# Reusing the maximum's turned score products as the first key tile, with one power of two per unit on GpSimd, in an attention and MLP block

## The chip, the cores and the metric

The kernel runs on one core of a Trainium2 chip. The metric is the device time of one execution in microseconds; the time of a kernel is the median of its runs.

## What is computed

The input `x` has 2048 tokens of width 448. The block adds three things: the input, an attention with 16 query heads of width 28 that share one key head and one value head, and an MLP of hidden width 1792. Both branches read the layer norm of `x`; the MLP normalizes once more.

```python
xn = _layernorm(x)
# attention: H = 16, Dh = 28, one k and one v for all heads
q = (xn @ wq).reshape(B, S, H, Dh).transpose(0, 2, 1, 3); k = xn @ wk; v = xn @ wv
scores = einsum("bhqd,bkd->bhqk", q, k) * Dh ** -0.5
o = einsum("bhqk,bkd->bhqd", softmax(scores), v)      # then heads side by side, @ wo
# MLP
y = _layernorm(xn); h = gelu(y @ w1 + b1); m = h @ w2 + b2
out = x + o @ wo + m
```

## The kernel before

The core has five engines with a queue each: PE multiplies matrices, ACT (ScalarE) evaluates functions, DVE (VectorE) and POOL (GpSimd) do elementwise work, SP (SyncE) issues most transfers. Each engine takes its own instructions strictly in the order in which the Python code issues them; semaphores make one engine wait for another. The schedule is written by hand: the loops call small jobs in turn.

There are three stages. First the norms and the projections to queries, keys and values; the queries go to DRAM (`qd`) as a high and a low part. Then the MLP, in slots of one 128-wide block of the hidden layer (`ft`) for 512 tokens (`c`), with the second product three slots behind the first. Last the attention, which begins some 354 us into the execution.

Attention is cut into 16 units. A unit is 512 queries of four heads (`j` = 0 to 3). The keys are cut into 16 tiles of 128 (`kt`). `score(u, kt, j)` makes one product of 128 keys by 512 queries on PE, into one of seven PSUM banks (`m`), and ACT takes the exponential of it into SBUF (`p`), so that keys lie on partitions. `pv(u, kt)` multiplies the four exponentials of a key tile by the values, into the one bank `po`, which also holds the sums of the exponentials (the values have a column of ones).

A unit takes eight steps, 0 to 7, of two key tiles. In a step the letters of a string say what is issued in turn: `s` a score, `m` a piece of work on maxima, `e` the end of that work, `n` a piece of the closing work of the unit before, `o` a piece of the output projection, `P` the value products of two key tiles (one step behind the scores).

The exponent needs a shift for each query, so that it doesn't overflow. The kernel uses the largest score over the first 128 keys. `max_jobs(u)` multiplies the queries of the unit by these keys (`km`) once more, as a product of its own: a score product of key tile 0, without the shift, since the rows that carry the shift are still empty. DVE turns each product in blocks of 32 by 32 (`tt`), and takes the largest of each block's rows (`mr`). `load_max(u)` joins the blocks, and SP sends the negative maxima, as a high and a low part, into two spare rows of the query tile `xh`. The score products then come out shifted. At the end `judge` looks whether all sums stayed in range; if not, a slow general path repeats the work (it is not taken with these inputs).

The closing work, `norm_jobs`, copies `po` to `oc`, squares it into a check sum, turns it, divides, and splits it into a high part `oth` (DVE) and a low part `otl` (POOL). The output projection of four units (`o_part`) reads these. Per unit there are 64 score products, 4 maximum products and the value products of 16 key tiles.

Of the kernel before, what the change touches and what calls it, by code (L numbers as in the profile page):

```python
# [15 lines left out]
P = 128  # L16
S, D, H, DH, F = 2048, 448, 16, 28, 1792
NT = S // P
CT = 4
# [4 lines left out]
EPS = 1e-5  # L24
SCALE = DH ** -0.5
BURST = 2
PAIRS = 12
# [11 lines left out]
def block_kernel(ctx, tc, x, wq, wk, wv, wo, w1, b1, w2, b2, out):  # L39
# [4 lines left out]
    def f(t):  # L44
        return t.bitcast(F32)
# [61 lines left out]
    def mtile(shape):  # L107
        return mp.tile(shape, F32, name="m")
# [344 lines left out]
    def load_q(u, blocks=range(4)):  # L453
        c, g = units[u]
        cols = slice(c * CW, (c + 1) * CW)
        if u < 2 and 0 in blocks:
            qst.append(xt_p.tile([P, 4, CW], F32R, name="xh"))
            pool.memset(f(qst[u]), 0.0)
# [9 lines left out]
    mrs = {}  # L468

# [9 lines left out]
    def load_max(u):  # L479
        while mxs.step():  # L480
            pass
        mb = mrs.pop(u)
# [10 lines left out]
        for h, r in ((0, 60), (1, 124)):  # L493
            for k in range(2):
                nc.sync.dma_start(f(qss[u][r:r + 1, 2 * k:2 * k + 2, :]), f(mn[:, h, k]))

    def max_jobs(u):
        mrs[u] = keep.tile([P, 4 * NT], F32, name="mr2", bufs=2)
        for j in range(4):
            pm = mtile([P, CW])  # L500
            pe.matmul(pm, km, qss[u][:, j, :], start=True, stop=True)  # L501
# [3 lines left out]
            dve.tensor_reduce(mrs[u][:, NT * j:NT * j + NT], tt.rearrange("p (b i) -> p b i", i=32), axis=AX.X, op=ALU.max)  # L505

# [15 lines left out]

    mxs, side, oside = Stream(), Stream(), Stream()

# [84 lines left out]
    ps = {}  # L609
    early = [(kt, j) for kt in range(2) for j in range(4)]  # L610

# [24 lines left out]
    for c in range(1, NCH):  # L636
        g = norm_gen(c, mtile)
        for i in range(CT + 1):
            norms[NF * (c - 1) + 5 + 2 * i] = lambda g=g: next(g, None)
    for n in range(len(mslots) + LAG):  # L640
        c, ft = mslots[n] if n < len(mslots) else (NCH, n - len(mslots))
# [10 lines left out]
        if (c, ft) == (NCH - 1, 7):  # L652
            load_q(0)
        if (c, ft) == (NCH - 1, 9):
            mxs.add(max_jobs(0))
        if (c, ft) == (NCH - 1, 12):
# [3 lines left out]
        for done, _ in enumerate(slot(n)):  # L660
            if done % 8 == 4 and (c, ft) in ((NCH - 1, 9), (NCH - 1, 10)):
                mxs.step()
            if c == NCH and done % 4 == 3 and early:
                score(0, *early.pop(0))
    assert not early
    ph1b.close()
# [15 lines left out]
    def prep_wo(g):  # L682
        pool.tensor_scalar(woh[:, g, :], wor[:, g, :], 1.0, 0.0, op0=ALU.mult, op1=ALU.add)
        pool.tensor_sub(wol[:, g, :], wor[:, g, :], f(woh[:, g, :]))

    rows = {}
# [140 lines left out]

    steps = [(u, kt) for u in range(NU) for kt in range(0, NT, 2)]
    pvq = [(u, kt) for u in range(NU) for kt in range(NT)]
    for n, (u, kt) in enumerate(steps):  # L830
        if n == len(steps) - 14:
            load_rows_of(NCH - 1, range(CT))
        if 4 <= n < 4 + NG:
            prep_wo(n - 4)
        if u and u + 1 < NU and kt == 0:
            load_q(u + 1)
        if u + 1 < NU and kt == 6:
            mxs.add(max_jobs(u + 1))
        jobs = [(u, kt + k, j) for k in range(2) for j in range(4)] if n else []
        for what in ORDERS[n % 2]:  # L840
            if what == "s" and jobs:
                score(*jobs.pop(0))
            elif what == "m":
                mxs.step()
            elif what == "e":
                if kt == 12 and u + 1 < NU:
                    load_max(u + 1)
            elif what == "n":
                side.step()
            elif what == "o":  # L850
                if n == len(steps) - 1:
                    o_part(NCH - 1, 0, range(NG - 1))
                oside.step()
            elif what == "P":
                assert not jobs
                for _ in range(BURST if n else 0):
                    pv(*pvq.pop(0))
    assert pvq and all(u == NU - 1 for u, kt in pvq)
# [6 lines left out]
    def full_max(u):  # L865
        qs = qst[u % 2]
        c, g = units[u]
# [19 lines left out]
    def general():  # L887
        for u in range(NU):
            c, g = units[u]
            full_max(u)  # L890
            qs = qst[u % 2]
            po = op.tile([P, CW], F32, name="po")
# [52 lines left out]
```

## Time and profile before

| | us |
|---|---|
| median of 3 runs | 913.89 (913.73 to 914.26) |
| the profiled execution | 913.37 |
| its span, first to last instruction | 911.4 |

| engine | busy us | share of the span |
|---|---|---|
| PE, matmuls | 900.5 | 99% |
| PE, weight loads | 583.5 | 64% |
| DVE | 428.6 | 47% |
| ACT | 712.7 | 78% |
| POOL | 61.2 | 7% |

A line of a group reads: source line, engine, operation, output <- inputs, shapes, count, then busy time and the mean duration of one in ns, then the engine's idle time just before them and what ended it. A line of the timeline reads: start in us, length in us, engine, line, operation, tiles, count; in brackets how long the engine had been idle and what released it. A line of the chain of waits has a start, a length and an engine with its line. PE's matmuls overlap one another, so a duration is more than the distance from one to the next; the same holds for ACT.

### The profile page before, as it was taken

Reading aid. Unit: us, or ns where it says so; the run is one execution under the profiler, and the core shown is the slowest. Engines: PE = TensorE matmul, PEld = TensorE weight load, DVE = VectorE, ACT = ScalarE, POOL = GpSimd, SP = SyncE. Lnnn points to the kernel's source line nnn. Section 1 sums busy time; section 2 is a strip of 40 time slices with the busy share of each in tenths; the row PEclk is TensorE's granted clock in tenths of the full one; section 3 lists DMA queues with packets and bytes.
Section 4 is the critical chain, followed back from the end, with each engine's and each line's share of the span. In section 5 each row is a group of like instructions: output and inputs, shape, how many; then the busy total and the mean of one; then the engine's idle time right before and its main releaser. Section 6 shows DMA issues by size and latency. Waiting matters only on the chain.

```text
span 911.4 us, 13365 instructions
## 1 busy us (share of the span) xinstructions
PE 900.5 (99%) x5041; PEld 583.5 (64%) x5041; DVE 428.6 (47%) x872; ACT 712.7 (78%) x1366; POOL 61.2 (7%) x69
## 2 busy tenths in 40 slices
PE   9999999999999999999999999999999999999997
PEld 8778888888888886444444564444564444564445
DVE  6777786676576584244234233234232244231212
ACT  5787664655554547999999969999969999969993
POOL 5340000000000002100000000000000000000000
PEclk9999999999999999999999999999999999999999
DMA  9773112002002204101102201102201102212001
GB/s 299 214 215 110 61 61 81 21 21 81 21 21 54 58 2 127 42 1 41 42 2 71 61 32 42 42 2 70 64 32 41 42 2 62 62 41 82 3 1 44
DMA packets 36265, 54.00 MB, mean 59 GB/s; under 512 B 7766, under 2 KB 24852, under 8 KB 36196
## 3 DMA queue, kind: packets, MB, share of 16 engines
q1 hardware_dynamic: 34788, 52.53, 19.9%
q8 instruction: 41, 0.67, 0.3%
q10 hardware_dynamic: 1408, 0.57, 0.2%
q14 instruction: 28, 0.23, 0.1%
HBM read 37.40 MB, written 14.68 MB: 57 GB/s over the span
## 4 chain that ended last, share of the span: by engine, by line
PE 95%; DVE 2%; DMA 1%; ACT 1%; issue 0%; SPq 0%; POOL 0%; DVEq 0%; POOLq 0%; ACTq 0%
PE m L630 28%; PE po L812 26%; PE ph L171 12%; PE m L573 5%; PE m L570 5%; PE m L576 5%; PE m L501 2%; PE qp L171 2%; PE m L703 1%; PE m L704 1%; PE m L705 1%; PE ph L174 1%; PE ph L176 1%; PE m L389 1%; PE m L263 1%; DMA qd<-qe 1%
## 5 line engine op out<-in xcount | busy, mean ns | idle before, releaser
L631 ACT ACTIVATE p<-m 128x512 f32<-128x512 f32 x1016 | 503.1, 666 | 39.2 <-PE m L630 38.8
L630 PE MATMUL m<-xh,ks 128*128 128x512 f32 x1024 | 276.7, 405 | 0.8 <-DVE a L580 0.8
L630 PEld LDWEIGHTS m<-xh,ks 128*128 128x128 f32 x1024 | 184.6, 188 | 118.7 <-ACT p L631 83.4
L812 PE MATMUL po<-p,vs 128*32 128x512 f32 x2016 | 242.4, 598 | 0.0
L812 PEld LDWEIGHTS po<-p,vs 128*32 128x32 f32 x2016 | 52.6, 109 | 119.0 <-issue 117.6
L740 DVE COPY oc<-po 128x512 f32<-128x512 f32 x15 | 10.4, 693 | 246.9 <-PE po L812 246.9
L544 ACT ACTIVATE hz<-ph,b1s 128x512 f32<-128x512 f32 x54 | 37.2, 689 | 103.4 <-PE ph L176 103.4
L576 PE MATMUL m<-w2h,hl 128*128 128x448 f32 x224 | 82.9, 370 | 0.0
L573 PE MATMUL m<-w2l,hh 128*128 128x448 f32 x224 | 82.0, 366 | 0.0
L570 PE MATMUL m<-w2h,hh 128*128 128x448 f32 x224 | 81.8, 365 | 0.0
L504 DVE STREAM_TRANSPOSE tt<-m 128x512 f32<-128x512 f32 x64 | 45.8, 716 | 67.5 <-PE m L501 64.5
L171 PE MATMUL ph<-xh,w1h 128*128 128x512 f32 x162 | 63.4, 391 | 0.8 <-ACT hx L545 0.8
L171 PE MATMUL ph<-xl,w1h 128*128 128x512 f32 x162 | 63.5, 392 | 0.3 <-DVE xl L265 0.3
L171 PE MATMUL ph<-xh,w1l 128*128 128x512 f32 x162 | 63.4, 391 | 0.0
L546 DVE TENSOR_SCALAR hz<-hz 128x512 f32<-128x512 f32 x56 | 25.3, 452 | 59.8 <-ACT hz L544 59.5
L755 POOL TENSOR_TENSOR otl<-oc,oth 128x512 fp32r<-128x512 f32 x15 | 19.4, 1292 | 484.8 <-PE m L630 274.0
L550 ACT ACTIVATE hz<-hz 128x512 f32<-128x512 f32 x56 | 35.3, 630 | 17.2 <-DVE hz L547 17.2
L570 PEld LDWEIGHTS m<-w2h,hh 128*128 128x128 f32 x224 | 42.1, 188 | 4.8
L573 PEld LDWEIGHTS m<-w2l,hh 128*128 128x128 f32 x224 | 42.1, 188 | 4.6
L505 DVE TENSOR_REDUCE mr<-tt 128x16 f32<-128x512 f32 x64 | 43.9, 686 | 2.2
L576 PEld LDWEIGHTS m<-w2h,hl 128*128 128x128 f32 x224 | 42.1, 188 | 3.3
L547 DVE TENSOR_TENSOR hz<-hz,hx 128x512 f32<-128x512 f32 x56 | 38.8, 693 | 7.7 <-ACT hx L545 4.9
(170 smaller groups left out, 968.2 us busy)
## 6 DMA issues: line engine op xcount, KB each, us to landing
xh<-qd SPq DMA_DIRECT2D x64, 224.0 KB
a<-in_A_x_dram SPq DMA_DIRECT2D x32, 224.0 KB
qd<-qe SPq DMA_DIRECT2D x24, 256.0 KB
ad<-a SPq DMA_DIRECT2D x16, 224.0 KB
a<-ad SPq DMA_DIRECT2D x16, 224.0 KB
raw<-in_B_w_dram SPq DMA_DIRECT2D x7, 448.0 KB
out_dram<-a SPq DMA_DIRECT2D x14, 224.0 KB
raw<-in_B_w_dram SPq DMA_DIRECT2D x4, 336.0 KB
```

The lines of the kernel that those rows point to most:

```text
L171: pe.matmul(ps, w, v, start=(n == 0), stop=False)
L504: dve.transpose(tt, pm)
L505: dve.tensor_reduce(mrs[u][:, NT * j:NT * j + NT], tt.rearrange("p (b i) -> p b i", i=32), axis=AX.X, op=ALU.max)
L544: act.activation(hz, ph, AF.Square, bias=b1s[:, ft:ft + 1], scale=GELU[0] ** 0.5)
L547: dve.tensor_mul(hz, hz, hx)
L550: act.activation(hz, hz, AF.Tanh, scale=GELU[1])
L570: pe.matmul(m2[k], hh[:, ts], w2h[:, ft, :], start=(ft == 0), stop=False)
L573: pe.matmul(m2[k], hh[:, ts], w2l[:, ft, :], start=False, stop=False)
L576: pe.matmul(m2[k], hl[:, ts], w2h[:, ft, :], start=False, stop=(ft == NF - 1))
L630: pe.matmul(s, ks[:, kt * P:(kt + 1) * P], qss[u][:, j, :], start=True, stop=True)
L631: act.activation(p, s, AF.Exp, scale=SCALE)
L812: pe.matmul(po[32 * j:32 * j + 32, :], vs[:, kt, :], ps.pop((u, kt, j)), start=(kt == 0), stop=(kt == NT - 1))
```

## The change

The maximum products of a unit are the scores of key tile 0, only without the shift and turned. The change keeps them in `tt` and makes the exponentials of key tile 0 from them, so that tile 0 is no longer scored a second time:

- `first_shift(u, j)`: DVE subtracts the maximum from the turned product, by a broadcast of `mq`, a copy of the maxima on all partitions that `load_max` now makes.
- `first_exp(u, j)`: ACT takes the exponential in place. For j = 0 of units 1 to 15 the shift is in powers of two (scaled by `BITS`, written to `bits`) and POOL raises a tile of twos to it.
- `first_back(u, j)`: DVE turns the result back into `p0`, which the value products of key tile 0 read.

Since maxima must be complete before the shift, they are now taken two units ahead (a third query tile is added), one maximum product in each of steps 3 to 6. These four steps have seven scores and the others eight (`SHARES`; a unit has 60). `shift_jobs(u + 1)` runs in steps 2 to 7 of unit u and in step 0 of the next, in the places `X` and `Y`. For unit 1 it starts a step later and ends in step 1 of unit 1, behind the first turn of unit 0's `norm_jobs`. Unit 0's exponentials of tile 0 are made in the MLP's last slots, all four on ACT.

On PE, over steps 2 to 4 of a unit before (L630 scores, L812 value products, L501 maximum products):

```order
L630 MATMUL m<-xh,ks 128x512 x8
L812 MATMUL po<-p,vs 32x512 x8
L501 MATMUL m<-xh,km 128x512
L630 MATMUL m<-xh,ks 128x512 x2
L501 MATMUL m<-xh,km 128x512
L630 MATMUL m<-xh,ks 128x512 x2
L501 MATMUL m<-xh,km 128x512
L630 MATMUL m<-xh,ks 128x512 x4
L812 MATMUL po<-p,vs 32x512 x8
L501 MATMUL m<-xh,km 128x512
L630 MATMUL m<-xh,ks 128x512 x8
L812 MATMUL po<-p,vs 32x512 x8
```

And on PE over steps 1 to 3 of a unit after (L683 scores, L875 value products, L510 maximum products; `p_4257` is the unit's tile p0):

```order
L683 MATMUL m<-xh,ks 128x512 x8
L875 MATMUL po<-p_4257,vs 32x512 x4
L875 MATMUL po<-p,vs 32x512 x4
L683 MATMUL m<-xh,ks 128x512 x8
L875 MATMUL po<-p,vs 32x512 x8
L683 MATMUL m<-xh,ks 128x512 x3
L510 MATMUL m<-xh,km 128x512
L683 MATMUL m<-xh,ks 128x512 x4
```

A maximum product now takes the place of a score, and the first four value products of a unit read tile 0 from p0. (One row of value products counts the eight instructions of the program; the trace shows each as two.)

On DVE, from the end of the closing work of a unit into its step 4, before:

```order
L751 TENSOR_TENSOR oc<-oc,tr 128x512 [waits DVE_49]
L753 CAST oth<-oc 128x512 [waits DVE_49]
L504 STREAM_TRANSPOSE tt<-m 128x512 [waits PE_49]
L505 TENSOR_REDUCE mr_4130<-tt 128x16 [waits DVE_49]
L504 STREAM_TRANSPOSE tt<-m 128x512 [waits DVE_49,PE_49]
L505 TENSOR_REDUCE mr_4130<-tt 128x16 [waits DVE_49]
```

And the same stretch after (L525 and L528 shifts, L517 and L518 turn and maximum of a maximum product, L540 the turn back into `p_4257`, the tile p0):

```order
L814 TENSOR_TENSOR oc<-oc,tr 128x512 [waits DVE_49]
L816 CAST oth<-oc 128x512 [waits DVE_49]
L525 SCALAR_TENSOR_TENSOR bits<-tt,mq 128x512
L528 TENSOR_TENSOR tt<-tt,mq 128x512
L517 STREAM_TRANSPOSE tt<-m 128x512 [waits PE_49]
L518 TENSOR_REDUCE mr_4221<-tt 128x16 [waits DVE_49]
L540 STREAM_TRANSPOSE p_4257<-tt 128x512 [waits Activation_49]
L528 TENSOR_TENSOR tt<-tt,mq 128x512
L517 STREAM_TRANSPOSE tt<-m 128x512 [waits PE_49]
```

The first two shifts follow the cast with no wait between; the third stands behind a turn that waits for ACT, and ahead of the next turn of a maximum product. The turn of the power's result (`p_4257<-bits`, waiting for POOL) stands at the end of the unit, ahead of the copy out of po.

On DVE in the MLP's last slots, before (L547 to L559 the MLP's own work, L651 a bias):

```order
L547 TENSOR_TENSOR hz<-hz,hx 128x512 [waits DVE_49,Activation_49]
L559 TENSOR_TENSOR hl<-hx,hh 128x512 [waits PE_49,Activation_49]
L551 TENSOR_SCALAR hz<-hz 128x512 [waits Activation_49]
L552 TENSOR_TENSOR hx<-hx,hz 128x512 [waits DVE_49]
L651 TENSOR_TENSOR a<-a,b2b 128x448 [waits DMAHW7_49,DMAHW3_49]
L559 TENSOR_TENSOR hl<-hx,hh 128x512 [waits PE_49,Activation_49]
```

And after (`xl` holds unit 0's turned products, `first` its tile p0):

```order
L599 TENSOR_SCALAR hz<-hz 128x512 [waits Activation_49]
L600 TENSOR_TENSOR hz<-hz,hx 128x512 [waits DVE_49,Activation_49]
L612 TENSOR_TENSOR hl<-hx,hh 128x512 [waits PE_49,Activation_49]
L528 TENSOR_TENSOR xl<-xl,mq 128x512 x2
L604 TENSOR_SCALAR hz<-hz 128x512 [waits Activation_49]
L605 TENSOR_TENSOR hx<-hx,hz 128x512 [waits DVE_49]
L540 STREAM_TRANSPOSE first<-xl 128x512
L528 TENSOR_TENSOR xl<-xl,mq 128x512
L540 STREAM_TRANSPOSE first<-xl 128x512 [waits Activation_49]
L706 TENSOR_TENSOR a<-a,b2b 128x448 [waits DMAHW7_49,DMAHW3_49]
L612 TENSOR_TENSOR hl<-hx,hh 128x512 [waits PE_49,Activation_49]
```

Two shifts, a turn, a shift and a turn now stand ahead of the last low part hl.

The diff, cut to its core:

```diff
-ORDERS = ("emnssmsnsmossssP", "emnssmsnsmossssP")
+BITS = SCALE * 1.4426950408889634
+ORDER = "YnssXsnMsosssseP"
+SHARES = (8, 8, 8, 7, 7, 7, 7, 8)
-    qs = qst[u % 2]
+    qs = qst[u % 3]
...
 def load_max(u):
-    while mxs.step():
-        pass
...
+    mqs[u] = keep.tile([P, 4 * NT], F32, name="mq", bufs=2)
+    for k in range(4):
+        dve.tensor_copy(mqs[u][32 * k:32 * k + 32], low)
+    if u:
+        dve.tensor_scalar(mqs[u][:, 0:NT], mqs[u][:, 0:NT], BITS, None, op0=ALU.mult)
-def max_jobs(u):
-    mrs[u] = keep.tile([P, 4 * NT], F32, name="mr2", bufs=2)
-    for j in range(4):
-        pm = mtile([P, CW])
-        pe.matmul(pm, km, qss[u][:, j, :], start=True, stop=True)
-        yield
-        tt = keep.tile([P, CW], F32, name="tt", bufs=1)
-        dve.transpose(tt, pm)
-        dve.tensor_reduce(mrs[u][:, NT * j:NT * j + NT], ..., axis=AX.X, op=ALU.max)
+def max_job(u, j):
...
+    pe.matmul(pm, km, qss[u][:, j, :], start=True, stop=True)
...
+    tts[u, j] = att.tile([P, CW], F32, name="tt", bufs=5)
+    dve.transpose(tts[u, j], pm)
+    dve.tensor_reduce(mrs[u][:, NT * j:NT * j + NT], blocks_of(tts[u, j]), axis=AX.X, op=ALU.max)
+def first_shift(u, j):
+    tt = blocks_of(tts[u, j])
+    shift = mqs[u][:, NT * j:NT * j + NT, None].to_broadcast([P, NT, 32])
+    if u and j == 0:
+        bits = att.tile([P, CW], F32, name="bits", bufs=1)
+        dve.scalar_tensor_tensor(blocks_of(bits), tt, BITS, shift, op0=ALU.mult, op1=ALU.subtract)
+        tts[u, j] = bits
+    else:
+        dve.tensor_tensor(tt, tt, shift, op=ALU.subtract)
+def first_exp(u, j):
+    if u and j == 0:
+        pool.tensor_tensor(tts[u, j], two, tts[u, j], op=ALU.pow)
+    else:
+        act.activation(tts[u, j], tts[u, j], AF.Exp, scale=SCALE)
+def first_back(u, j):
+   ...
+    dve.transpose(p0s[u][:, j], tts.pop((u, j)))
+    ps[u, 0, j] = p0s[u][:, j]
+def shift_jobs(u):
+    first_shift(u, 0)
+    first_exp(u, 0)
+    yield
+    yield
+    for j in range(1, 4):
+        first_shift(u, j)
+        yield
+        first_exp(u, j)
+        yield
+        first_back(u, j)
+    for _ in range(4):
+        yield
+    first_back(u, 0)
-early = [(kt, j) for kt in range(2) for j in range(4)]
+early = [(1, j) for j in range(4)]
+firsts = {(NCH - 1, 13): {12: "s0", 14: "x0 s1", 16: "b0", 18: "x1 s2", 20: "b1"},
+          (NCH, 0): {2: "x2 s3", 5: "b2", 8: "x3", 11: "b3"}}
...
+two = att.tile([P, CW], F32, name="two", bufs=1)
+pool.memset(two, 2.0)
...
+todo = [(u, kt, j) for kt in range(1 if u else 2, NT) for j in range(4)]
+        if i == 0 and u + 2 < NU:
+            load_q(u + 2)
+        jobs = todo[:SHARES[i] if u else 8 * (i > 0)]
+        maxima = [(u + 2, i - 3)] if 3 <= i < 7 else []
+        if u == 0 and i in (1, 2):
+            maxima = [(1, 2 * i - 2), (1, 2 * i - 1)]
+                elif what == "M":
+                    for v, j in maxima:
+                        if v < NU:
+                            max_job(v, j)
+                elif what in "XY":
+                    if what == "X" and i == (2 if u else 3) and u + 1 < NU:
+                        xside.add(shift_jobs(u + 1))
+                    xside.step()
+                elif what == "e":
+                    if i == 7 and u + 2 < NU:
+                        load_max(u + 2)
+                    if n == 2:
+                        load_max(1)
```

More of the change, by code (lines that the diff above doesn't have):

```diff
@@ L661, in block_kernel @@
             if done % 8 == 4 and (c, ft) in ((NCH - 1, 9), (NCH - 1, 10)):
-                mxs.step()
-            if c == NCH and done % 4 == 3 and early:
+                if len(tts) < 4:
+                    max_job(0, len(tts))
+            if (c, ft) in firsts and done in firsts[c, ft]:
+                for job in firsts[c, ft][done].split():
+                    dict(s=first_shift, x=first_exp, b=first_back)[job[0]](0, int(job[1]))
+            if c == NCH and done % 8 == 7 and early:
                 score(0, *early.pop(0))
+    for kt, j in early:
+        score(0, kt, j)
+    early.clear()
     assert not early
@@ L826, in o_wait @@
         yield from o_jobs(c)
-    steps = [(u, kt) for u in range(NU) for kt in range(0, NT, 2)]
+    xside = Stream()
     pvq = [(u, kt) for u in range(NU) for kt in range(NT)]
[L830 to L857, printed above, removed]
```

53 lines of the change are left out of this document (44 added, 9 removed).

## The prediction, made before the changed kernel was run

> **What bounds the kernel now.** I read the page first (busy shares, slices, chain), then the chain of waits over one unit, then the timeline at the places that the change touches.
>
> ```profile
> PE 900.5 (99%) x5041; PEld 583.5 (64%) x5041; DVE 428.6 (47%) x872; ACT 712.7 (78%) x1366; POOL 61.2 (7%) x69
> PEld 8778888888888886444444564444564444564445
> ACT  5787664655554547999999969999969999969993
> PE 95%; DVE 2%; DMA 1%; ACT 1%; issue 0%; SPq 0%; POOL 0%; DVEq 0%; POOLq 0%; ACTq 0%
> L631 ACT ACTIVATE p<-m 128x512 f32<-128x512 f32 x1016 | 503.1, 666 | 39.2 <-PE m L630 38.8
> L630 PE MATMUL m<-xh,ks 128*128 128x512 f32 x1024 | 276.7, 405 | 0.8 <-DVE a L580 0.8
> L546 DVE TENSOR_SCALAR hz<-hz 128x512 f32<-128x512 f32 x56 | 25.3, 452 | 59.8 <-ACT hz L544 59.5
> L550 ACT ACTIVATE hz<-hz 128x512 f32<-128x512 f32 x56 | 35.3, 630 | 17.2 <-DVE hz L547 17.2
> ```
>
> Attention fills the right half. PE and ACT both look full there, so the page doesn't say which sets the pace. The chain of waits over one unit (start, us, what) does:
>
> ```profile
> 561.09 2.04 PE m L630 x8
> 563.12 1.85 PE po L812 x16
> 564.98 0.43 PE m L501
> ...
> 567.81 1.85 PE po L812 x16
> 569.67 0.43 PE m L501
> 570.10 1.83 PE m L630 x8
> 571.93 1.85 PE po L812 x16
> 573.78 2.07 PE m L630 x8
> 575.85 1.85 PE po L812 x16
> 577.71 2.04 PE m L630 x8
> ...
> 593.33 2.04 PE m L630 x8
> ```
>
> The pieces join without a hole and all are PE's. A plain step (eight score products, two key tiles of value products) is 573.78 to 577.71, 3.9 us. The two steps that also carry four maximum products last 564.98 to 573.78, 8.80 us, against 7.8 for two plain ones: 1.0 us for four products, 0.25 each. In the step from 569.67 nine products take 0.43 + 1.83 = 2.26 where eight take 2.05: 0.21 for the ninth. ACT, from the timeline:
>
> ```profile
> 570.37 30.12 ACT L631 ACTIVATE p<-m 128x512 f32<-128x512 f32 x61 [0.66 <-PE m L630]
> 525.46 2.06 ACT L631 ACTIVATE p<-m 128x512 f32<-128x512 f32 x4 [1.29 <-PE m L630]
> ```
>
> Over a long run one exponential starts every (30.12 - 0.67) / 60 = 0.49 us, but a burst of four behind a PE delay goes at (2.06 - 0.67) / 3 = 0.46. Eight cost ACT about 3.7 to 3.8 us, and the step gives it 3.9: ACT is paced by PE with 0.1 us to spare.
>
> **The change, part by part.**
>
> *64 score products go (four for each of 16 units).* The maximum products stay, 64 as before, one a step now instead of three and one. Steps 3 to 6 hold 7 + 1 products and the others 8, so a plain unit should be eight plain steps, 8 x 3.9 = 31.2, where it is 32.24 now (window below). At 0.21 to 0.25 each the 64 give 13.4 to 16.0 us; I take 15, near the 0.25, since the whole-unit figure says 1.0.
>
> ```profile
> 561.09:593.33 32.24, 32.24 (x197) 15.47 (x197) 10.98 (x23) 31.55 (x66) 1.30 (x1) 1.00 0.14 30
> ```
>
> (Columns: length, then busy us of PE, weight loads, DVE, ACT, POOL; the granted clock is 1.00.)
>
> *ACT* has 63 exponentials a unit instead of 64; three read SBUF (the 0.63 us of L550 against 0.67 for L631), and no step has more than eight. It stays just under PE: no cost. If it were not, each step would lose what it is over; I bound that by 0 and 0.1 us a step.
>
> *DVE* gains four shifts and four turns a unit, and the copies of the maximum. The same forms stand at the head of a unit:
>
> ```profile
> 589.55 0.69 DVE L740 COPY oc<-po 128x512 f32<-128x512 f32 x1 [16.50 <-PE po L812]
> 590.27 0.69 DVE L722 SCALAR_TENSOR_TENSOR sq<-oc 128x512 f32<-128x512 f32 x1
> 590.89 0.71 DVE L745 STREAM_TRANSPOSE tr<-oc 128x512 f32<-128x512 f32 x1
> 591.41 1.92 PE L812 MATMUL po<-p,vs 128*32 128x512 f32 x16
> 591.63 0.25 DVE L747 RECIPROCAL rc<-tr 128x16 f32<-128x16 f32 x1
> 592.66 0.69 DVE L751 TENSOR_TENSOR oc<-oc,tr 128x512 f32<-128x512 f32 x1
> 593.39 0.43 DVE L753 CAST oth<-oc 128x512 fp32r<-128x512 f32 x1
> 593.99 1.29 POOL L755 TENSOR_TENSOR otl<-oc,oth 128x512 fp32r<-128x512 f32 x1 [30.95 <-PE m L630]
> ```
>
> 4 x 0.69 + 4 x 0.71 + about 1 = 6.6 us on the 10.98 of the window: 17.6 of 31. The load fits beside PE; its cost is zero as long as no instruction waits at the head of DVE's queue, because the turn of each maximum product stands in that queue and frees one of PE's seven banks. That cover is the third rival's subject.
>
> *GpSimd's power* is in no row. Below it stands the 1.29 us of L755, the same shape with a subtraction. Above, I let a power be thirty elementary passes (my assumption) of the kind of L683:
>
> ```profile
> 361.22 0.57 POOL L683 TENSOR_SCALAR woh<-wor 128x448 fp32r<-128x448 f32 x1 [6.33 <-DMA wor<-in_A_wo_dram]
> ```
>
> 0.57 x 512 / 448 x 30 = 19.5 us. Between 1.3 and 20 the geometric middle is 5 us; a logarithm and an exponential lie above a subtraction, so I take 7. What hides it: the result is turned only at the end of the unit (DVE's row from bits), six steps after it begins, so even 20 us is hidden, if nothing else waits for GpSimd. The otl subtraction queued behind it is next wanted by a copy 6 steps later.
>
> What may wait is DVE. The trace has two places where it did:
>
> ```profile
> 53.10 1.64 POOL L320 TENSOR_TENSOR w1l<-raw,w1h 128x672 fp32r<-128x672 f32 x1 [2.78 <-issue]
> 54.01 0.77 DVE L190 SCALAR_TENSOR_TENSOR rs<-rs 128x16 f32<-128x16 f32 x1
> ...
> L190 DVE SCALAR_TENSOR_TENSOR rs<-rs x6: 164/166/773, 6.2 to 54.0; 128x4 f32<-128x4 f32 x3, 128x2 f32<-128x2 f32 x2, 128x16 f32<-128x16 f32 x1
> 341.41 1.81 POOL L458 MEMSET xh<- 128x2048 f32 x1 [69.28 <-PE ph L174]
> 342.33 1.17 DVE L546 TENSOR_SCALAR hz<-hz 128x512 f32<-128x512 f32 x1
> ```
>
> L190, with two SBUF inputs, usually 0.166 us, took 0.77 and ended at 54.78, just after GpSimd's 54.74. L546, on average 0.45, took 1.17, to 0.28 past the memset's end. So a DVE instruction of these kinds stands still until GpSimd's instruction is over. The shifts have two SBUF inputs. In the unit shown, whose step 2 starts at 593.33 on PE: the cast ends at 593.82, the first shift at 594.51, and the second, right behind it with no wait, at 595.20; the power starts then. The third shift follows the turn of exponential 1, which ACT reaches at the start of step 4 (593.33 + 2 x 3.9 = 601.1): 601.1 + 0.67 + 0.71 = 602.5. It must end before ACT wants it at the start of step 5, 605.05, so it can wait until 604.35. Hence a power up to 604.35 - 595.20 = 9.1 us costs nothing. With my 7 it is over before the third shift even asks (7.3).
>
> The Trainium skill says of this, in the page "SBUF — State Buffer", section "Who interferes with whom", that the pair of SBUF ports that VectorE shares with GpSimd is an exclusive lock held for a whole instruction, and that an instruction with two SBUF inputs contends with a GpSimd instruction that reads SBUF. The two places above agree with it (0.77 for 0.166 us); by it a power of any length blocks the shift to its end, and if instead the port were shared the sum would stand for a long power too.
>
> *What is moved.* Queries are loaded and maxima sent a unit earlier, in the same number on SP's queue (four and four a unit), so each has some 30 us more to land: no cost. GpSimd first clears a third query tile (1.81 us, as L458 above) and fills the constant; the tile's first product comes three steps, 12 us, later. The output weights' split now stands behind unit 1's power; its first reader is in unit 5. Unit 1's maxima come two a step in steps 1 and 2, where DVE has nothing else. Any of these late would be a wait of a few microseconds once; I put them at nothing.
>
> *Two costs that come once.* In the MLP's tail DVE gets two shifts, a turn, another shift and a turn ahead of the last split (hl): 3 x 0.69 + 2 x 0.71 = 3.5 us.
>
> ```profile
> 346.85 0.69 DVE L559 TENSOR_TENSOR hl<-hx,hh 128x512 fp32r<-128x512 f32 x1 [0.17 <-ACT hh L557]
> 350.55 0.36 PE L576 MATMUL m<-w2h,hl 128*128 128x448 f32 x1
> ```
>
> hl is ready at 347.5 now and used at 350.55; then 351.0, with PE some 0.7 us earlier because scores have gone: PE waits about 1.2 (0 to 2.5). And for unit 1 the turn of the power's result stands behind the copy, the square and the first turn of unit 0's sums, so it ends as if at 591.63 + 0.71 = 592.3 where its value products would start at 591.41: 0.9 us. Together 2.1.
>
> *Sum:* 15 - 2.1 = 12.9 us. The profiled execution took 913.37 us (span 911.4), 0.5 under the median of 913.89. 913.4 - 12.9 = 900.5, so 901 for the median, 1.4% faster. Own range of this case: 16.0 saved, no wait, and the 0.8 us that PE idles before the first score of attention gone too (row L630 of PE) give 897; 13.4 saved, 2.5 lost in the tail and 2 at unit 1 give 905.
>
> **The rivals.**
>
> *ACT sets the step.* For it: ACT's row of 61 exponentials has no hole, at 0.49 each, and the weight loads are busy at 4 tenths in attention. Then a unit gains only the exponential that leaves ACT: 15 x 0.49 = 7.4 us, less 2.1: 5.3, so 909. Against it: the chain stays on PE, and the bursts of four run at 0.46. The Trainium skill (page "Trainium Kernel Development and Optimization", section "Performance Expectations") calls matmul busy time a bad measure and weight-load busy time a good one; by that rule PE, loading weights for 15.47 of 32.24 us, isn't the bound, and this rival holds. Here the seamless chain speaks against it.
>
> *GpSimd's power holds DVE (slower).* Place: the third shift of each unit. Beyond 9.1 us each further microsecond holds the shift, ACT's exponential behind it, and the turn that frees PE's bank: PE, whose third product of step 5 needs that bank, is stopped nearly as long. 11 units have this spacing; in the three with output projections the steps are longer and the free length is about 11 us. The gain of 12.9 is eaten at 9.1 + 12.9 / 11 = 10.3 us. A power of 12 us costs 11 x 2.9 + 3 = 35 (936), of 15 us 77 (978). For it: a power is far from a subtraction. Against it: everything I know of its length is the bracket.
>
> *The products go and PE idles instead.* If the later turns and shifts free banks late, by 0.9 us a unit, the saving comes back as waits on DVE and the time is 912 to 915. For it: one turn a step now waits behind ACT's exponential. Against it: in step 4 the turn ends at 602.5 + 0.69 + 0.72 = 603.9, and its bank is wanted seven products on, by the third of step 5, at 605.05 + 3 x 0.25 - 0.25 = 605.6.
>
> **How the numbers follow.** Chances: forecast 0.50; ACT sets the step 0.12; given back 0.07; power too long 0.31. The last: spread evenly in the logarithm from 1.3 to 20 us, 24 in 100 lie beyond 10.3 us; I raise it because a power must be several times a subtraction. A measurement of this kernel tells about 0.2% (1.8 us) from no change. Faster by more than that: the first two, 0.62. Within it 0.07. Slower 0.31. The range starts at 897; of the long powers six tenths lie beyond 13.2 us (901 + 11 x 4.1 + 3 x 2.2 = 953), 0.19, so it reaches to 953.
>
> **What the profile will show.** Right: plain units of 31.2 to 31.4 us from one copy out of po to the next; 15 powers; GpSimd's row of them under 9 us; chain still PE. Wrong: third shifts far over 0.69 us, ending with the power, and PE idle released by DVE or ACT at step 5 (the power holds DVE); weight loads waiting for DVE's turns (given back); ACT without a hole and PE with holes (ACT). A tail wait over 2.5 us would break the one-time sum.

## The result, and the profile after

| kernel | median us | lowest to highest | ratio to before, 95% interval |
|---|---|---|---|
| before, on the same chip | 913.85 | 913.73 to 914.26 | |
| after | 1741.89 | 1741.04 to 1742.74 | 1.906 (1.9027 to 1.9093) |

The change makes the kernel nearly twice as slow. The forecast was 901. The page of the profile after the change (busy times, slices, chain, three groups):

```profile
PE 911.8 (52%) x4977; PEld 575.8 (33%) x4977; DVE 522.8 (30%) x1079; ACT 707.0 (41%) x1351; POOL 1299.5 (75%) x86
POOL 4200000069998989898989898989898989899990
PEclk9999999995767676676867676758585858595859
POOL 68%; PE 19%; issue 5%; DVE 5%; DMA 2%; ACT 1%; SPq 0%; DVEq 0%; POOLq 0%; ACTq 0%
L532 POOL TENSOR_TENSOR bits<-two,bits 128x512 f32<-128x512 f32 x15 | 1235.8, 82384 | 76.3 <-DVE bits L525 76.3
L540 DVE STREAM_TRANSPOSE p<-bits 128x512 f32<-128x512 f32 x15 | 10.7, 711 | 914.9 <-POOL bits L532 914.9
L875 PE MATMUL po<-p,vs 128*32 128x512 f32 x2016 | 262.8, 642 | 652.1 <-DVE oc L803 594.7
```

The group of L532 says nearly all of it: fifteen powers of 82.4 us each, 1235.8 us of GpSimd, where PE needed 32.25 us for a whole unit. PE has lost its place in the chain to POOL (95% of it before, 19% now). DVE's turn of the power's result waits 914.9 us in all, and PE's value products 594.7 us for the copy out of `po`.

The timeline shows how one power hands over to the next (start, length, engine, instruction, idle time before it and its releaser):

```profile
546.89 82.49 POOL L532 TENSOR_TENSOR bits<-two,bits 128x512 f32<-128x512 f32 x1 [5.05 <-DVE bits L525]
629.36 1.26 POOL L818 TENSOR_TENSOR otl<-oc,oth 128x512 fp32r<-128x512 f32 x1
629.42 0.71 DVE L540 STREAM_TRANSPOSE p<-bits 128x512 f32<-128x512 f32 x1 [62.45 <-POOL bits L532]
630.66 0.69 DVE L803 COPY oc<-po 128x512 f32<-128x512 f32 x1 [0.53 <-POOL otl L818]
631.40 3.56 PE L875 MATMUL po<-p,vs 128*32 128x512 f32 x16 [55.82 <-DVE oc L803]
...
634.50 0.43 DVE L816 CAST oth<-oc 128x512 fp32r<-128x512 f32 x1
634.84 0.68 DVE L525 SCALAR_TENSOR_TENSOR bits<-tt,mq 128x512 f32<-128x512 f32 x1
635.44 0.68 DVE L528 TENSOR_TENSOR tt<-tt,mq 128x512 f32<-128x512 f32 x1
635.67 82.49 POOL L532 TENSOR_TENSOR bits<-two,bits 128x512 f32<-128x512 f32 x1 [5.05 <-DVE bits L525]
644.07 0.65 DVE L528 TENSOR_TENSOR tt<-tt,mq 128x512 f32<-128x512 f32 x1
648.01 0.65 DVE L528 TENSOR_TENSOR tt<-tt,mq 128x512 f32<-128x512 f32 x1
```

This is a ring. When the power ends, GpSimd makes the `otl` that was queued behind it (1.26 us), and DVE the turn of the power. Only then the copy out of `po` can run: it overwrites `oc`, which that `otl` reads, and it stands behind the turn in DVE's queue. The closing work follows, then the next unit's shift, and the next power. From one power's start to the next are 635.67 - 546.89 = 88.78 us: 82.5 of power and 6.3 of the rest. The unit time is the ring, and PE is only a passenger:

```profile
575.00:629.00 54.00, 0.58 (x3) 0.15 (x1) 0.00 (x0) 3.06 (x7) 54.00 (x1) 0.55 0.00 1
629.00:635.00 6.00, 3.60 (x17) 0.70 (x17) 4.88 (x10) 0.00 (x0) 1.62 (x2) 0.52 0.00 0
635.00:650.00 15.00, 15.00 (x94) 7.26 (x96) 7.72 (x12) 14.57 (x30) 14.33 (x1) 1.00 0.00 1
```

(Windows: length, then busy us of PE, weight loads, DVE, ACT and POOL, each with its number of instructions; then the granted clock.) PE stands still for 54 us, and its first 16 value products behind that take 3.56 us at a granted clock of 0.52, where they took 1.92 before.

The last two rows of the timeline matter for the rivals. The third and fourth shifts (L528, 644.07 and 648.01) run at 0.65 us while the power is under way: it does not hold them. All 34 shifts of this trace that lie wholly inside a power took 0.65 to 0.69 us.

### The profile page after: what moved, and what is told of

It reads as the page before. It is cut to its first block, busy times and chain, and to the rows that moved or that the text cites. A ratio compares the mean times of both kernels' runs of the same rounds, so it can differ in the third digit from the quotient of the medians.

```text
span 1740.5 us, 13396 instructions
## 1 busy us (share of the span) xinstructions
PE 911.8 (52%) x4977; PEld 575.8 (33%) x4977; DVE 522.8 (30%) x1079; ACT 707.0 (41%) x1351; POOL 1299.5 (75%) x86
## 4 chain that ended last, share of the span: by engine, by line
POOL 68%; PE 19%; issue 5%; DVE 5%; DMA 2%; ACT 1%; SPq 0%; DVEq 0%; POOLq 0%; ACTq 0%
POOL bits L532 66%; PE ph L173 6%; PE m L629 2%; PE m L626 2%; PE m L623 2%; PE po L875 1%; POOL otl L818 1%; PE ph L176 1%; PE ph L178 1%; PE m L683 1%; PE qp L173 1%; DVE oc L803 1%; DVE bits L525 1%; DVE sq L785 0%; DVE oc L814 0%
## 5 line engine op out<-in xcount | busy, mean ns | idle before, releaser
L532 POOL TENSOR_TENSOR bits<-two,bits 128x512 f32<-128x512 f32 x15 | 1235.8, 82384 | 76.3 <-DVE bits L525 76.3
L684 ACT ACTIVATE p<-m 128x512 f32<-128x512 f32 x956 | 482.3, 670 | 871.1 <-PE m L683 870.7
L875 PE MATMUL po<-p,vs 128*32 128x512 f32 x2016 | 262.8, 642 | 652.1 <-DVE oc L803 594.7
L875 PEld LDWEIGHTS po<-p,vs 128*32 128x32 f32 x2016 | 55.1, 114 | 783.7 <-DVE oc L803 599.3
L540 DVE STREAM_TRANSPOSE p<-bits 128x512 f32<-128x512 f32 x15 | 10.7, 711 | 914.9 <-POOL bits L532 914.9
L683 PE MATMUL m<-xh,ks 128*128 128x512 f32 x960 | 271.7, 411 | 1.5 <-DVE a L633 1.5
L683 PEld LDWEIGHTS m<-xh,ks 128*128 128x128 f32 x960 | 172.0, 189 | 147.8 <-ACT p L684 88.6
L461 POOL MEMSET xh<- 128x2048 f32 x3 | 5.4, 1811 | 271.3 <-PE ph L176 202.1
L768 PE MATMUL m<-woh,otl 128*128 128x448 f32 x64 | 24.4, 381 | 161.6 <-POOL otl L818 161.6
L768 PEld LDWEIGHTS m<-woh,otl 128*128 128x128 f32 x64 | 12.3, 192 | 163.6 <-POOL otl L818 162.8
L517 DVE STREAM_TRANSPOSE tt<-m 128x512 f32<-128x512 f32 x60 | 42.2, 703 | 51.7 <-PE m L510 51.3
L540 DVE STREAM_TRANSPOSE p<-tt 128x512 f32<-128x512 f32 x45 | 32.0, 712 | 80.5 <-ACT tt L534 80.5
```

What stands on the lines that cost most here:

```text
L517: dve.transpose(tts[u, j], pm)
L532: pool.tensor_tensor(tts[u, j], two, tts[u, j], op=ALU.pow)
L540: dve.transpose(p0s[u][:, j], tts.pop((u, j)))
L683: pe.matmul(s, ks[:, kt * P:(kt + 1) * P], qss[u][:, j, :], start=True, stop=True)
L684: act.activation(p, s, AF.Exp, scale=SCALE)
L768: pe.matmul(po, otl[:, ts], woh[:, g, :], start=False, stop=(g == NG - 1))
```

## The experiments

Each kernel ran beside the kernel before, on the same chip as its batch; its median was 913.6 to 913.75. "Unit" is the distance between two copies out of `po` in units without output projection (32.25 before). "First copy" is the start of the first of these copies, so it holds the costs of the start of attention (386.38 before).

| kernel | median us | ratio, 95% interval | unit | first copy |
|---|---|---|---|---|
| e1_act4 | 910.41 | 0.9957 (0.9943 to 0.9970) | 31.48 | 395.43 |
| e2_sub | 906.53 | 0.9918 (0.9905 to 0.9932) | 31.25 | 393.32 |
| e3_junk | 909.97 | 0.9961 (0.9948 to 0.9974) | 31.48 | 394.89 |
| e4_64 | 908.06 | 0.9935 (0.9914 to 0.9955) | 31.43 | 391.48 |
| e11_128 | 908.64 | 0.9942 (0.9924 to 0.9960) | 31.36 | 392.97 |
| e10_192 | 979.07 | 1.0715 (1.0696 to 1.0735) | 37.61 | 392.92 |
| e7_spread | 908.09 | 0.9938 (0.9924 to 0.9951) | 31.47 | 392.41 |
| e8_query | 904.38 | 0.9901 (0.9886 to 0.9916) | 31.47 | 389.19 |
| e9_tail | 905.23 | 0.9909 (0.9894 to 0.9924) | 31.47 | 389.40 |
| e12_128q | 905.68 | 0.9913 (0.9895 to 0.9930) | 31.36 | 391.28 |

### The power alone

**The power on ACT** (e1_act4): everything of the change but the place of one exponential.

```
-            pool.tensor_tensor(tts[u, j], two, tts[u, j], op=ALU.pow)
+            act.activation(tts[u, j], tts[u, j], AF.Exp, scale=0.6931471805599453)
```

> The power goes to ACT as a fourth exponential (of the same shifted bits, scaled by ln 2); nothing else differs from the changed kernel. Theory (the power's 82 us in a ring through POOL is the whole loss): 901 us, 897 to 905, plain units of 31.2 to 31.4 us with POOL idle, since the sum of the prediction without the power is left. Rival 1 (ACT sets the step): 64 exponentials a unit again, no gain over the kernel before, 909 to 914. Rival 2 (turns and shifts in DVE's queue hold PE's banks): over 914, with weight loads waiting for DVE.

910.41, 0.4% faster than before. All of the 830 us hang on that one line: from the first copy out of `po` to the last there are 1304.5 us in the kernel after and 469.9 here, and these 834.6 with a first copy 3.8 us earlier in the kernel after account for the loss. The 901 expected here was missed, and the first rival's window of 909 to 914 was met; the next kernels show that only part of the miss is ACT's.

The trace shows one thing more. GpSimd is free now when the closing work comes, and its subtraction meets the second shift:

```profile
630.57 1.58 POOL L818 TENSOR_TENSOR otl<-oc,oth 128x512 fp32r<-128x512 f32 x1 [29.91 <-PE m L683]
630.91 1.79 DVE L528 TENSOR_TENSOR tt<-tt,mq 128x512 f32<-128x512 f32 x1
```

The shift takes 1.79 us instead of 0.65, and ends 0.55 us after the subtraction. It is so in all 11 units with this spacing. A subtraction on GpSimd does hold the very instruction that the power leaves alone.

**A subtraction in the power's place** (e2_sub). It leaves out the exponential of key tile 0 for one head of each unit, so its output isn't the block's; only its time is of use.

```
-            pool.tensor_tensor(tts[u, j], two, tts[u, j], op=ALU.pow)
+            pool.tensor_tensor(tts[u, j], two, tts[u, j], op=ALU.subtract)
```

> POOL subtracts instead of raising to a power (same tiles, same place, 1.3 us), so key tile 0 of head 0 of each unit is wrong in value. Theory: 901 us, like the kernel with four exponentials on ACT, within 2 us of it. If ACT sets the step, this one is faster than that by 15 x 0.48 = 7 us. If any wait on POOL in this place were the trouble, whatever its length, it stays far above 914.

906.53, and units of 31.25 us: what the prediction said of a plain unit if GpSimd's part is hidden (31.2). With the power's duration at 1.5 us the schedule does what it was drawn for. So it is the duration, not the order of the work. The kernel with all four exponentials on ACT needs 31.48 a unit; the 0.23 us between the two is ACT's, which has 64 exponentials at 0.49 us there and 63 here. With 63, ACT waits for PE once a unit:

```profile
583.99 19.21 ACT L684 ACTIVATE p<-m 128x512 f32<-128x512 f32 x39 [0.22 <-PE m L683]
```

One exponential more, 0.49 us, is 0.27 more than this wait holds, near the 0.23. The held shift above is not the reason: in e3_junk and e7_spread no shift is held, and their units take 31.48 and 31.47. That the median is still 5.5 us above 901 lies mostly in the start of attention, below.

**Four powers that nobody reads** (e3_junk): the power on ACT as above, `otl` on DVE so that nothing needed is queued behind GpSimd, and in four units a full power into a tile of its own.

```
-        pool.tensor_sub(otl, oc, f(oth))
+        dve.tensor_sub(otl, oc, f(oth))
...
+            if i == 3 and u in (1, 4, 7, 10):
+                junk = att.tile([P, CW], F32, name="junk", bufs=1)
+                pool.tensor_tensor(junk, two, two, op=ALU.pow)
```

> As the kernel with four exponentials on ACT, with the closing subtraction (otl) moved to DVE so that nothing waits for POOL, and four powers of full size started in units 1, 4, 7 and 10 whose results nobody reads: POOL runs powers for 330 us beside everything else. Theory (a running power doesn't hold DVE): within 3 us of the same kernel without them, 900 to 906 us, shifts at 0.65 to 0.70 us inside the powers. Port rival (each power holds the first shift that meets it until its end): 4 x 70 us or so more, about 1180.

Groups and timeline of this kernel (two powers fill GpSimd from 369.34 to 533.37):

```profile
L906 POOL TENSOR_TENSOR junk<-two 128x512 f32<-128x512 f32 x4 | 327.8, 81947 | 0.2
369.34 164.03 POOL L906 TENSOR_TENSOR junk<-two 128x512 f32<-128x512 f32 x2
440.69 0.65 DVE L528 TENSOR_TENSOR tt<-tt,mq 128x512 f32<-128x512 f32 x1
444.63 0.65 DVE L528 TENSOR_TENSOR tt<-tt,mq 128x512 f32<-128x512 f32 x1
472.17 0.65 DVE L528 TENSOR_TENSOR tt<-tt,mq 128x512 f32<-128x512 f32 x1
```

328 us of power cost nothing: 909.97 against 910.41, units 31.48 in and out of the powers. DVE's shifts, with two SBUF inputs, take 0.65 us in the middle of a power, the same as without one. So a running power doesn't hold DVE's shifts. Only at its very start something is held, a scaling of `mq` that begins 0.12 us behind the first power and takes 0.95 us where others take 0.18:

```profile
369.46 0.95 DVE L501 TENSOR_SCALAR mq<-mq 128x16 f32<-128x16 f32 x1
```

A copy 0.15 us behind the second power's start took 1.02. Otherwise a power costs only through those who wait for its result or stand behind it. The power of 2 by 2 takes 81.9 us and that of real exponents 82.4, so the length hardly depends on the numbers. The kernel with `otl` on DVE but without the extra powers was not run, so a small gain of that move could hide an equally small cost; a hold of 82 us could not hide.

### The length of the power

**64, 128 and 192 of the 512 columns** (e4_64, e11_128, e10_192): GpSimd raises the first columns, ACT the others.

```
-            pool.tensor_tensor(tts[u, j], two, tts[u, j], op=ALU.pow)
+            pool.tensor_tensor(tts[u, j][:, 0:64], two[:, 0:64], tts[u, j][:, 0:64], op=ALU.pow)
+            act.activation(tts[u, j][:, 64:CW], tts[u, j][:, 64:CW], AF.Exp, scale=0.6931471805599453)
```

> POOL raises only 64 of the 512 columns, ACT does the other 448. Theory: the power costs 82.4 x 64 / 512 = 10.3 us, hidden in the six steps (23 us) before its result is turned: 901 to 905 us. If a running power holds DVE's shifts (the port rival), the third shift waits 1 to 2 us a unit: 912 to 930, and third shifts longer than 0.7 us in the timeline. If the power's time doesn't go with the columns: far over 1000.

> POOL raises 192 of the 512 columns, ACT does the rest of that exponential, turn at the unit's end as in the changed kernel. By the 10.8 us of 64 columns and the 82.4 of 512, 31.3 us a power. Theory (a power is hidden up to about 26 us, from its shift in step 2 to the copy out of po at the end of the next unit's step 0; beyond that the unit is the power, the closing subtraction of 1.3 us and the 5.05 us of turn, closing work and shift in a ring): units of 37.7 us, 14 x 6.3 = 88 us over 908: 990 to 1000. Rival (GpSimd is only a throughput limit, 31.3 + 1.3 a unit): units of 32.6, about 925.

> Power on 128 of the 512 columns on GpSimd, the other 384 on ACT. At the measured 0.163 us a column the power takes 20.8 us, as long as the upper end of the prediction's bracket (19.5). Theory of the unit's ring (power, turn, copy out of po, closing work, shift, the next power: the power's length and 6.4 us more, as 37.6 for 31.2 with 192 columns): 20.8 + 6.4 = 27.2 us, under the 31.4 that PE and ACT need, so the power is hidden, plain units of 31.35 to 31.43 us and 907.5 us (906 to 909.5). Rival, the prediction's own: a running power holds DVE's shifts to its end. The third shift is then held 20.8 - 9.1 = 11.7 us in each of 11 units, units of about 43 us, and 908 + 129 = 1037 (1000 to 1050).

The groups of the power in the three kernels, in this order:

```profile
L532 POOL TENSOR_TENSOR bits<-two,bits 128x64 f32<-128x64 f32 x15 | 161.6, 10772 | 302.2 <-ACT p L685 242.4 <-DVE bits L525 59.8
```

```profile
L532 POOL TENSOR_TENSOR bits<-two,bits 128x128 f32<-128x128 f32 x15 | 314.9, 20995 | 161.6 <-ACT p L685 147.5 <-DVE bits L525 14.1
```

```profile
L532 POOL TENSOR_TENSOR bits<-two,bits 128x192 f32<-128x192 f32 x15 | 468.1, 31206 | 80.6 <-DVE bits L525 61.4 <-ACT p L685 19.3
```

With the 82.38 us of 512 columns the four lie on a line: (82.38 - 10.77) / 448 = 0.160 us a column and 0.5 us besides, which gives 21.0 for 128 and 31.2 for 192.

At 10.8 and 21.0 us the power is hidden in the plain units (31.43 and 31.36, the second shorter because ACT's part of the exponential has 384 columns instead of 448). With 128 columns PE waits 1.8 us once for unit 1's turn, 1.0 more than with 64. The 901 to 905 expected of 64 columns was missed by 3 us, with the first copy 5.1 later than before. By the rival in which a power holds DVE, 21 us would have made 1037; it made 908.64. At 192 columns the ring of the kernel after is back, from one power's start to the next:

```profile
786.07 31.29 POOL L532 TENSOR_TENSOR bits<-two,bits 128x192 f32<-128x192 f32 x1 [5.08 <-DVE bits L525]
817.33 1.26 POOL L819 TENSOR_TENSOR otl<-oc,oth 128x512 fp32r<-128x512 f32 x1
817.39 0.71 DVE L541 STREAM_TRANSPOSE p<-bits 128x512 f32<-128x512 f32 x1 [10.52 <-POOL bits L532]
818.63 0.69 DVE L804 COPY oc<-po 128x512 f32<-128x512 f32 x1 [0.52 <-POOL otl L819]
823.67 31.30 POOL L532 TENSOR_TENSOR bits<-two,bits 128x192 f32<-128x192 f32 x1 [5.08 <-DVE bits L525]
```

823.67 - 786.07 = 37.6 us, 31.3 and the same 6.3. The total of 979 is 11 to 21 us less than I expected, partly because the units with an output projection do not get longer (39.1 on average, 40.95 with 128 columns): their PE work lies beside the power. So the free length ends between 21 us and 31, at 31.4 - 6.3 = 25 us if the ring holds there too; no kernel was run at that point.

### What was left at the start of attention

In e2_sub the 14 distances from the first to the last copy out of `po` add up to 467.2 us (480.4 before), 13.2 less; but the first copy comes 6.9 us later, and the end after the last copy is 0.7 shorter. Sum 7.0, the difference of the spans (911.4 and 904.4). Waits of PE from 340 to 400 us in e2_sub (total, times, longest), and the clock behind the first of them:

```profile
PE m L510 <- DMA xh<-qd: 2.0, 1, 2.0
PE m L683 <- DVE a L633: 1.4, 1, 1.4
PE m L629 <- DVE hl L612: 1.1, 1, 1.1
PE po L875 <- DVE rc L810: 0.8, 1, 0.8
368.00:374.00 6.00, 6.00 (x27) 2.77 (x27) 2.26 (x4) 3.51 (x7) 5.67 (x7) 0.72 0.01 1
```

The kernel before has only the wait for `a` there, 0.8. Of the 6.9 us, 2.2 lie ahead of the first value product (356.05 before, 358.30 here). In them are the wait for `hl` and 0.6 more for `a`, and 0.7 that arises ahead of anything the change touches: the MLP's first product starts at 66.08 us before and at 66.74 here, after work that is the same in both. In the twelve profiled executions that start lies between 66.0 and 67.5, without relation to the edits, so differences of a microsecond between two traces can come from there. The last 4.7 lie between the first value product and the first copy: 2.0 for `xh`, 0.8 for the turn (`rc` stands for DVE's queue), 1.0 for four more maximum products, since unit 0 now makes those of units 1 and 2, and 0.9 more, where the clock is lower. The experiments take up the first, the `xh` and the `hl`, on the kernel with all exponentials on ACT.

**The shifts spread evenly** (e7_spread): the first shift no longer begins in step 2 with its exponential in a step of eight scores, and its turn follows at once.

```
-        first_shift(u, 0)
-        first_exp(u, 0)
-        yield
-        yield
-        for j in range(1, 4):
+        for j in range(4):
             first_shift(u, j)
             yield
             first_exp(u, j)
             yield
             first_back(u, j)
-        for _ in range(4):
-            yield
-        first_back(u, 0)
```

> All four exponentials on ACT, with the first one moved from step 2, where ACT then has nine, to step 3, which has only seven scores, and its turn right behind it instead of at the unit's end. Theory (one step of nine exponentials costs the 0.22 us a unit by which plain units with four on ACT, 31.47, lie above those with POOL's subtraction, 31.25): units of 31.25 again, 15 x 0.22 = 3.3 us less than 910.4, and 0.8 us less since unit 1's late turn goes: 906 to 907. Rival (64 exponentials are too many wherever they stand): 909.5 to 911.

908.09, 2.3 less than with the same exponentials in the old order. The expected return of the units to 31.25 did not come: they stay at 31.47, so 64 exponentials are too many wherever they stand. The first copy comes 3.0 us earlier. Behind the wait for `xh` PE isn't stopped again there: ACT has one exponential less in that step, and unit 1's turn is no longer late.

**The third query tile loaded earlier** (e8_query).

```
+    load_q(2)
     wor = att.tile([P, NG, D], F32, name="wor", bufs=1)
...
-            if i == 0 and u + 2 < NU:
+            if i == 0 and 0 < u and u + 2 < NU:
                 load_q(u + 2)
```

> As the one before, and the third query tile (unit 2's) is cleared and loaded ahead of the output weights instead of behind them. Theory (PE's wait of 2.0 us for that load in unit 0, and the lower clock that follows the wait in some executions, are the largest one-time cost): that wait goes, 2 to 4.5 us less, 902 to 904.5, and less spread between runs. Rival (the load isn't late because of its place): no change.

Waits of PE in this kernel from 340 to 400 us:

```profile
PE m L676 <- DVE a L626: 1.4, 1, 1.4
PE m L622 <- DVE hl L605: 1.1, 1, 1.1
PE m L676 <- ACT p L677: 0.3, 1, 0.3
```

The wait for `xh` is gone, and time with it: 904.38, the lowest median of this study and 1.0% under the kernel before. That is 3.7 us less for a wait of 2.3. The two traces differ by 4.0: 2.2 lie between the first value product and the first copy, where the wait was; 1.0 lies ahead of the MLP's first product (67.19 and 66.20) and 0.8 behind the last copy, and that these two belong to the edit is not shown. **The same move with 128 columns on GpSimd** (e12_128q) brought 3.0 us:

> The kernel of 128 columns with the third query tile loaded ahead of the output weights, so that unit 2's first product doesn't wait for it (2.0 to 2.3 us of PE, in the kernels without the power's length). If only this wait goes: 2.1 us less than with 128 columns alone, 905.4 (904 to 907). In the spread kernel it brought 3.7 us, because the clock stayed up too and the first copy out of po came 3.2 us sooner: then 904 (902.5 to 905). Rival: the query's load was not the cause and another wait takes its place: no change.

905.68 against 908.64. The wait of 2.4 us for `xh` went, and the wait for unit 1's turn fell from 1.8 to 0.9.

**The MLP's tail** (e9_tail), on top of e8_query: unit 0's shifts and exponentials in the first slots of the tail, its turns only behind the tail, so that nothing of them stands ahead of `hl`.

```
-    firsts = {(NCH - 1, 13): {12: "s0", 14: "x0 s1", 16: "b0", 18: "x1 s2", 20: "b1"},
-              (NCH, 0): {2: "x2 s3", 5: "b2", 8: "x3", 11: "b3"}}
+    firsts = {(NCH, 0): {1: "s0", 2: "x0 s1", 3: "x1 s2", 4: "x2 s3", 5: "x3"}}
...
     early.clear()
+    for j in range(4):
+        first_back(0, j)
```

> As the one before, and in the MLP's tail the shifts of unit 0 come behind the last low part hl and the turns behind the last sums, ahead of the maximum work of unit 1. Theory (PE waits 1.1 to 1.5 us for hl because of the shifts and turns ahead of it): that wait goes, 1 to 1.5 us less, 901 to 903. Rival (the turns now hold the first scores or the first value products instead): no change or up to 3 us more.

A miss: 905.23, no better than 904.38. The waits of PE in the same stretch:

```profile
PE m L676 <- ACT p L677: 1.3, 2, 1.0
PE m L510 <- DMA xh<-qd: 0.7, 1, 0.7
PE m L676 <- ACT first L677: 0.7, 1, 0.7
```

The waits for `hl` (1.1) and `a` (1.4) went, and 2.7 us of others came, against 2.8 before this edit. So the tail's wait was handed on to ACT's exponentials and to the query, which was late again. Its tile's clearing on GpSimd waits for the turns that now stand behind the tail:

```profile
355.26 1.81 POOL L461 MEMSET xh<- 128x2048 f32 x1 [11.94 <-DVE first L540]
```

In e8_query the same clearing began at 353.57.

## Why the prediction was wrong

**The step that failed** is the upper end of the bracket for GpSimd's power: "let a power be thirty elementary passes (my assumption) of the kind of L683", 19.5 us. Measured: 82.4 us, 126 passes of that kind (0.57 x 512 / 448 = 0.65 us each). There was no row near it, and the prediction treated its own assumption as an end of the range. The value taken, 7 us, was a middle between that end and a subtraction, so it inherited the error: 82.4 is twelve times it. How GpSimd works a power out, and so why it takes this long, no run here shows. The range to 953 and the chance of 0.31 for slower followed from the same bracket. The place of the failure was named beforehand, "everything I know of its length is the bracket"; its size was not.

**"Even 20 us is hidden"** was right in the plain units: 21.0 us cost nothing there, and about 1 us once at unit 1. The end of the cover, 25 us by the ring, could have been worked out from the schedule. The power begins in step 2 of one unit and its turn ends the unit; with that, 82 us could have been priced as (82.5 + 6.3 - 31.25) for each plain unit. The prediction priced long powers only by another mechanism.

**That mechanism, the power that holds DVE, was wrong**; that this rival's verdict (slower) came true is luck. The two places in the trace of before, an instruction of 0.166 us that took 0.77 and one of 0.45 that took 1.17, are of GpSimd's subtraction and memset. (The 0.166 is a median of mostly smaller shapes; L191, next to it and of its own shape, takes 0.18, so the reading stands.) A subtraction does hold a shift, 1.79 us for 0.65 in e1_act4. It does not carry over to the power: shifts at 0.65 us inside it, 328 us of powers without loss. The Trainium skill says, in the page "SBUF — State Buffer", section "Who interferes with whom", that the shared pair is held for a whole instruction, and that a DVE instruction with two SBUF inputs contends with a GpSimd instruction that reads SBUF. For the subtraction the trace of e1_act4 agrees. For the power the runs show otherwise, and the measurement decides. Whether the power leaves the ports between its columns, no run here shows.

**The saving on PE** was right. "Eight plain steps, 8 x 3.9 = 31.2": 31.25 measured in e2_sub. From the first copy out of `po` on, 13.2 and 0.7 us came, inside the range of 13.4 to 16.0 that the prediction gave the saving.

**"It stays just under PE: no cost"**, said of ACT, held with 63 exponentials a unit (31.25), and so did the reading of the chain against the rival in which ACT sets the step. With 64 ACT sets it: 31.48, and 31.43, 31.36 and 31.25 as the 64th shrinks to 448, 384 and no columns. The margin was one exponential wide. The rule that the prediction weighed there, matmul busy time as a bad measure (the Trainium skill, page "Trainium Kernel Development and Optimization", section "Performance Expectations"), would, as the prediction applied it, have had PE not the bound in e2_sub either, where weight loads are busy for about 15 us of a unit; its units are PE's 31.25.

**The one-time costs** were mis-sized: 2.1 foreseen, 6.9 measured at the first copy, of which 0.7 arises ahead of anything the change touches; so 6.2. The two that were named came as named (`hl` 1.1 for 1.2, unit 1's turn 0.8 for 0.9). Of what was put "at nothing", the third query tile came 2.0 late. "The tile's first product comes three steps, 12 us, later" counted from its clearing, but its loads stood behind those of the output weights: with them ahead, in e8_query, the wait was gone. Against it stand also the four maximum products that moved ahead of the first copy (1.0), and 0.6 at the first score, where the prediction let the idle 0.8 us stay or go, not grow. With a short power, 901 would have been 901 + 6.2 - 2.1 = 905 for this alone, and 906 with the saving at 13.9 for 15; e2_sub took 906.53.

## What to carry to other kernels

An operation without a row has no upper bound until it is measured; an assumed number of passes is not a bound, and when the whole case hangs on it, the schedule's free length (here 25 us a unit) should be worked out first and the chance put on either side of that. An engine that is busy only 7% of the time can become the bound the moment one long instruction joins a ring with queues of other engines: count the ring, not the load. Loads that are moved need their wait looked at where they are first used: here taking away a wait of 2.3 or 2.4 us brought 3.7 and 3.0 us by the medians, and not all of that is shown to be the wait's.

## What the runs showed of the hardware

- GpSimd's power of two tensors takes 0.160 us a column of 128 partitions (10.8, 21.0, 31.2 and 82.4 us for 64, 128, 192 and 512), nearly the same for constant operands (81.9). ACT does 512 columns of an exponential at one in 0.49 us.
- A power under way does not slow DVE's instructions with two SBUF inputs (0.65 us, 34 of 34 in the kernel after). A subtraction of the same shape does (1.79 us in e1_act4). In e3_junk two small DVE instructions that began 0.12 and 0.15 us behind a power's start took 0.95 and 1.02 us for 0.18.
- The clock granted to PE was lower around PE's long stops: 0.55 over a stop of 54 us, 0.52 over the next 6 us, in which 16 value products took 3.56 us. Behind the stop of 2.0 us in e2_sub it was 0.50 for 3.41 us. In e7_spread PE waited 2.3 us at the same place, and the products behind it kept to 1.92. The traces show a difference between the two (first two rows e2_sub, last two e7_spread):

```profile
364.65:368.07 3.42, 1.38 (x6) 0.85 (x6) 2.44 (x12) 1.64 (x4) 0.62 (x1) 1.00 0.29 64
368.07:371.48 3.41, 3.41 (x13) 1.39 (x15) 1.97 (x3) 2.56 (x5) 3.24 (x4) 0.50 0.01 1
363.05:366.46 3.41, 2.87 (x20) 0.90 (x19) 3.27 (x6) 3.08 (x8) 3.05 (x4) 1.00 0.81 196
366.46:369.87 3.41, 1.70 (x10) 1.18 (x14) 3.27 (x8) 1.55 (x4) 3.24 (x5) 1.00 0.04 6
```

In all twelve traces the clock changes only at whole multiples of 3.413 us from the start of its record: in e2_sub the record starts at 6.25, and 106 such stretches later, at 368.07, the clock falls. In e2_sub the whole stop lies in one stretch (3.42 - 1.38 = 2.04 us idle), and the clock is down in the next. In e7_spread, whose record starts at 4.65, a border at 366.46 cuts the stop in two (0.54 and 1.71), and the clock stays up. While PE still has work, every fall in the twelve traces follows a stretch with at least 1.83 us of idle PE, and no stretch of full clock with 1.78 or less was followed by one. So where the stop lies between the borders fits all that was seen; no experiment moved it on purpose.
